# The first load of q in two pieces, and blank matmuls of twice the width

## The chip, the core and the metric

The kernel runs on one core of a Trainium2 chip. A core has engines that work side by side, each with its own queue of instructions: TensorE (PE in the profile; its weight loads are PEld), VectorE (DVE), ScalarE (ACT), GpSimd (POOL) and SyncE (SP), which issues most of the transfers between the chip's main memory and the on-chip memory. Engines wait for each other, and for transfers, by semaphores. The metric is the device time of one execution in microseconds.

## The reference

The program is a linear attention ("cosformer") and then a two-layer network with a leaky ReLU. Batch is 8, heads 8, sequence 576, head size 64, so 4608 tokens of 512 values enter the network; its inner width is 2048.

```python
def phi(x, c, s):                       # c, s: cosine and sine of the position
    r = np.maximum(x, 0.0)
    return np.concatenate([r * c, r * s], axis=-1)
q_p, k_p = phi(q, cos_w, sin_w), phi(k, cos_w, sin_w)
kv  = np.einsum('bhsf,bhsd->bhfd', k_p, v)
z   = np.sum(k_p, axis=2)
num = np.einsum('bhsf,bhfd->bhsd', q_p, kv)
den = np.einsum('bhsf,bhf->bhs', q_p, z)[..., None] + 1e-06
x   = (num / den).transpose(0, 2, 1, 3).reshape(4608, 512)
h   = x @ w_in
out = np.maximum(0.01 * h, h) @ w_out
```

## The kernel before

**Tiles and stages.** For each batch element the first 512 positions lie as 128 partitions by 4 positions (the "main" part); the remaining 64 positions of all elements are gathered into a ninth group of 512 tokens. For each group the kernel builds phi of q and k (DVE and ACT, `phi_half`, L237), turns q round so that its features lie on the partitions (`q_transpose`, L362, in PSUM by TensorE for the first groups), multiplies k with v (`kv_mm`, L285; a column of ones in v gives z), multiplies q with that (`num_half`, L408) and divides (`divide`, L390). The result is turned round again (`x_transpose_half`, L424) and goes through the two layers of the network. The first layer of group 0 is `ffn1` (L451), its second `ffn2` (L470). From group 1 on the network's matmuls are split by a Strassen-like scheme with seven products in place of eight, and the next groups' attention runs between them at positions that tables at the end of the kernel give (L1066 to L1075).

**What sets the order.** The program is written out by hand: each engine carries out its instructions in the order in which the Python code issues them. There is no scheduler that moves them. Before group 1 that order is plain code, L147 to L609.

**The start.** SP issues, in this order, q's first four heads, q's last four, then k's first four, v's first four, k's last, v's last (each 512 KB, `load_main`, L88), and eight loads of the first layer's weights (`load_w1`, L135). The 64 tail positions of k and v go through POOL's queue (L210, L211). The transfers that SP issues use eight semaphores in turn; the ninth waits until the first has landed, and so on.

DVE sets a tile `blank` to zero (L162). `idle(n, ps)` (L166) issues 2n matmuls of that tile, 128 by 128, with itself, 256 columns wide, into a PSUM tile that the next real matmul overwrites or that nobody reads. Their result is zero and is used nowhere: they keep TensorE busy. The kernel calls `idle` in these places:

- L171, 14 (28 matmuls): before anything has landed
- L562, 1 each: behind the eight transposes of q's positions 0 and 1
- L572, 14: inside `kv_half(0, 0)`, before the first matmuls of k and v (tile `ps_kvh`)
- L577, 2: inside the first `num_half` (tile `ps_numh`)
- L586, 2: inside `kv_half(0, 1)`

Between these, DVE and ACT make phi of q from the tile `qst` into `qp` (L239 and L241), four heads at a time: first for the heads of q's first load, then for those of its second. TensorE transposes `qp` (L366), eight heads for each of four positions; DVE and ACT copy that to `qpT` (L247, L249). Then follow phi of k (`kpm`), v (`vmain`) and the matmuls of the two (L290, L299), ACT's copy of them to `kv` (L323), the products with q (L417), the division (L392 to L397) and the transposes of the result (L434).

The line numbers are those of the kernel before; in the changed kernel the lines behind L88 stand two further down and those behind L168 five further down.

Of the kernel before, what the change touches and what calls it, by code (L numbers as in the profile page):

```python
# [13 lines left out]
P = 128  # L14
J = 4
# [3 lines left out]
def kernel(  # L19
# [14 lines left out]
    nc = tc.nc  # L34
# [4 lines left out]
    MAIN = J * P  # L39
# [6 lines left out]
    N2 = MAIN // 2  # L46
# [29 lines left out]
    def psum(where, shape, dtype, name):  # L76
        return ps_of[where].tile(shape, dtype, name=name, tag="ps_" + where)

    st = {}
# [4 lines left out]
    def staged(shape, name, soon=False):  # L84
        p, tag = (early, "early") if soon else (stage, "stage")
        return p.tile(shape, dt.float32, name=name, tag=tag)

    def load_main(nm, src, b, parts=(0, 1), soon=False):  # L88

        if parts[0] == 0:  # L90
            st[nm, b] = staged([P, H, J, D], f"{nm}st", soon)
        lo, hi = 4 * parts[0], 4 * parts[-1] + 4
        nc.sync.dma_start(
            st[nm, b][:, lo:hi],
            src[b, lo:hi, 0:MAIN, :].rearrange("h (p j) d -> p h j d", j=J),
        )

    def load_kvtail(nm, src, b, eng=nc.sync):

# [15 lines left out]
    def load_k(b):  # L115
        load_main("k", k, b)
        load_kvtail("k", k, b)

    def load_v(b):
        load_main("v", v, b)  # L120
        load_kvtail("v", v, b)
# [20 lines left out]
    def load_w2(i):  # L142
        t = staged([P, 4, DM], "w2st", i > 1)
        nc.sync.dma_start(t, w2v[i])
        st["w2", i] = t

    load_main("q", q, 0, (0,))  # L147
    load_main("q", q, 0, (1,))
    load_main("k", k, 0, (0,))
    load_main("v", v, 0, (0,))  # L150
# [10 lines left out]
    blank = const.tile([P, N2], dt.float16, name="blank")  # L161
# [2 lines left out]
    nc.scalar.activation(warm, zero, AF.Sin)  # L164

    def idle(n, ps):  # L166
        for _ in range(2 * n):
            nc.tensor.matmul(ps[:, 0:N2], lhsT=blank[:, 0:P], rhs=blank)  # L168

    ps_idle = psum("s", [P, 2, MAIN], dt.float32, "ps_idle")[:, 0]  # L170
    idle(14, ps_idle)  # L171


# [144 lines left out]
    def kv_half(b, hg, where, blanks=0):  # L318
        ps = psum(where, [P, MAIN], dt.float32, "ps_kvh")
        idle(blanks, ps)  # L320
        ps = ps[:, 0 : 4 * NE]
        kv_mm(b, hg, ps)
        nc.scalar.copy(  # L323
            kv[b][:, 4 * hg : 4 * hg + 4, 0 : NE - 1],
            ps.rearrange("p (h e) -> p h e", h=4)[:, :, 0 : NE - 1],
        )
# [81 lines left out]
    def num_half(g, jp, hg, where, blanks=0):  # L408

        if hg == 0:  # L410
            st["xp", g, jp] = qppool.tile([P, 2, H, D], dt.float16, name="xp", tag="qp")
        ps = psum(where, [P, 2, 512], dt.float32, "ps_numh")
        idle(blanks, ps[:, 0])
        for o in range(2):
            for hh in range(4):
                h = 4 * hg + hh
                nc.tensor.matmul(  # L417
                    ps[:, o, hh * NE : (hh + 1) * NE - 1],
                    lhsT=st["qpT", g, 2 * jp + o][:, h, :],
                    rhs=kv[g][:, h, 0 : NE - 1],  # L420
                )
        divide(ps, st["xp", g, jp][:, :, 4 * hg : 4 * hg + 4, :])
# [243 lines left out]
    ps = psum("n", [P, 2, DM], dt.float32, "ps_o")  # L666
# [22 lines left out]
    ps = psum("h", [P, 2, MAIN], dt.float16, "ps_x")  # L689
# [360 lines left out]
    step = length[2] / 28  # L1050
# [109 lines left out]
```

## Time and profile before

| | |
|---|---|
| median of 3 runs | 271.99 us (271.53 to 272.37) |
| the profiled execution | 271.19 us |
| its span, first to last instruction | 269.4 us |
| PE busy | 263.5 us, 98% of the span |
| DVE busy | 203.8 us, 76% |
| ACT busy | 199.4 us, 74% |
| POOL busy | 13.1 us, 5% |
| first landing of q waited for by DVE until | 4.56 us |

The profile is of one execution. In a row of the timeline the first number is the start in microseconds from the start of the span, the second the time from the first of a group's instructions to the end of its last; then come engine, line, operation, what it writes and reads, its shape, how many there are, and in brackets how long the engine had been idle before and what ended that. SPq is SP's queue: such a row is the issue of a transfer, not the transfer. Matmuls are pipelined: one of 256 columns takes 272 ns from its start to its end, while the next starts 0.11 us after it; so the distance of their starts is what counts. In a row of a tile's transfers, "to landing" is counted from the start of the issue.

### The profile page before, as it was taken

How to read it: one execution, taken by the hardware profiler on the slowest of the kernel's cores; microseconds unless marked ns; L12 is line 12 of the kernel's file. 1: busy time of each engine (PE TensorE's matmuls, PEld its weight loads, DVE VectorE, ACT ScalarE, POOL GpSimd, SP SyncE). 2: the span in 40 equal slices, each digit the busy share in tenths (PEclk: the TensorE clock that was granted, in tenths of full speed). 3: DMA queues.
4: the chain of work that ended last, by engine and by line, in shares of the span. 5: the costliest groups of instructions: out<-in, count | busy, mean ns of one | idle time of the engine just before them, and what ended most of it. 6: DMA issues, size and time to landing. Idle time of an engine off the chain costs nothing.

```text
span 269.4 us, 6623 instructions
## 1 busy us (share of the span) xinstructions
PE 263.5 (98%) x2670; PEld 227.0 (84%) x2670; DVE 203.8 (76%) x452; ACT 199.4 (74%) x329; POOL 13.1 (5%) x25
## 2 busy tenths in 40 slices
PE   8999999999999999999999999999999999999994
PEld 6985455665998989899999999999999899999983
DVE  5875798797967898888879778977687758545652
ACT  8757476696888896978888788878877757666720
POOL 5047001000000000000000000000000000000000
PEclk9999999999999999999999999999999999999999
DMA  6999999979999979958995899669384412200324
GB/s 226 373 392 415 393 386 373 357 170 296 274 252 313 191 195 249 354 116 285 259 254 122 271 239 247 156 202 154 62 142 155 61 41 97 80 0 2 156 41 117
DMA packets 86190, 57.05 MB, mean 212 GB/s; under 512 B 55632, under 2 KB 81232, under 8 KB 85648
## 3 DMA queue, kind: packets, MB, share of 16 engines
q1 hardware_dynamic: 85584, 55.98, 77.0%
q8 instruction: 21, 0.34, 0.6%
q10 hardware_dynamic: 448, 0.39, 0.4%
q0 software_dynamic: 128, 0.26, 0.3%
q14 instruction: 9, 0.07, 0.1%
HBM read 36.70 MB, written 9.44 MB: 171 GB/s over the span
## 4 chain that ended last, share of the span: by engine, by line
PE 76%; DVE 2%; issue 0%
PE ps_o L883 33%; PE ps_h L782 30%; PE ps_h L496 4%; PE ps_num L381 3%; PE ps_h L883 3%; PE ps_kv L290 2%; DVE gs L255 0%; PE ps_kv L299 0%; PE ps_xt L446 0%; DVE xs L397 0%; DVE w L255 0%; DVE wb L255 0%; DVE ob L252 0%; DVE qp L241 0%; DVE kpt L241 0%
## 5 line engine op out<-in xcount | busy, mean ns | idle before, releaser
L883 PEld LDWEIGHTS <-g 128*128 128x128 f16 x648 | 62.7, 98 | 7.2 <-DVE g L252 0.3
L252 DVE TENSOR_TENSOR u<-ps_h,u 128x512 f32<-128x512 f32 x52 | 35.8, 688 | 21.0 <-PE ps_h L782 19.3
L883 PE MATMUL ps_o<-w,g 128*128 128x256 f16 x352 | 51.2, 273 | 0.0
L782 PEld LDWEIGHTS <-w 128*128 128x128 f16 x416 | 44.7, 113 | 1.2
L782 PE MATMUL ps_h<-xT,w 128*128 128x256 f16 x288 | 43.3, 273 | 0.0
L809 ACT ACTIVATE g<-u 128x1024 f16<-128x1024 f32 x26 | 27.5, 1058 | 11.2 <-DVE u L252 10.9
L802 ACT COPY u<-ps_h 128x512 f32<-128x512 f32 x52 | 30.5, 586 | 7.1 <-PE ps_h L782 7.0
L795 ACT ACTIVATE g<-ps_h 128x512 f16<-128x512 f32 x52 | 31.2, 602 | 5.6 <-PE ps_h L782 5.6
L782 PEld LDWEIGHTS <-wa 128*128 128x128 f16 x312 | 33.7, 113 | 1.2
L883 PE MATMUL ps_o<-wb,g 128*128 128x256 f16 x232 | 33.5, 273 | 0.0
L782 PE MATMUL ps_h<-xw,wa 128*128 128x256 f16 x208 | 31.3, 273 | 0.0
L883 PEld LDWEIGHTS <-gs 128*128 128x128 f16 x256 | 24.9, 98 | 2.9
L901 ACT COPY ob<-ps_o 128x512 f32<-128x512 f32 (+1 forms) x32 | 18.1, 565 | 11.9 <-PE ps_o L883 10.6
L496 PE MATMUL ps_h<-xT,w 128*128 128x512 f16 (+1 forms) x104 | 24.7, 363 | 0.0
L397 DVE TENSOR_TENSOR xs<-ps_num,rden 128x512 f16<-128x512 f32 x28 | 19.4, 691 | 1.0
L883 PE MATMUL ps_o<-w,gs 128*128 128x256 f16 x120 | 17.8, 273 | 0.0
L252 DVE TENSOR_TENSOR ob<-ps_o,ob 128x512 f32<-128x512 f32 (+1 forms) x22 | 14.9, 675 | 3.8 <-ACT ob L901 1.9
L883 PE MATMUL ps_o<-wb,gs 128*128 128x256 f16 x120 | 17.5, 273 | 0.0
L792 ACT COPY ps_h<-ps_h 128x512 f32<-128x512 f32 x26 | 14.9, 572 | 2.4 <-PE ps_h L782 1.5
L255 DVE TENSOR_TENSOR gs<-g 128x1024 f16<-128x1024 f16 x16 | 11.0, 688 | 7.3 <-ACT g L809 7.2
L782 PE MATMUL ps_h<-xw,w 128*128 128x256 f16 x104 | 15.6, 273 | 0.0
L782 PE MATMUL ps_h<-xT,wa 128*128 128x256 f16 x104 | 15.6, 273 | 0.0
(116 smaller groups left out, 411.8 us busy)
## 6 DMA issues: line engine op xcount, KB each, us to landing
qst<-in_q_dram SPq DMA_DIRECT2D x7, 1024.0 KB, 6.4
out_dram<-ob SPq DMA_DIRECT2D x14, 512.0 KB, 2.8
kst<-in_k_dram SPq DMA_DIRECT2D x6, 1024.0 KB, 7.1
vst<-in_v_dram SPq DMA_DIRECT2D x6, 1024.0 KB, 7.2
w1st<-in_moe_w_in_dram SPq DMA_DIRECT2D x8, 512.0 KB, 10.5
w2st<-in_moe_w_out_dram SPq DMA_DIRECT2D x4, 1024.0 KB, 12.3
kst<-in_k_dram SPq DMA_DIRECT2D x4, 512.0 KB, 8.1
vst<-in_v_dram SPq DMA_DIRECT2D x4, 512.0 KB, 8.3
```

The lines of the kernel that those rows point to most:

```text
L252: nc.vector.tensor_tensor(out=o, in0=a, in1=b, op=ALU.add)
L255: nc.vector.tensor_tensor(out=o, in0=a, in1=b, op=ALU.subtract)
L381: nc.tensor.matmul(ps[lo:hi, h // 4, (h % 4) * NE : (h % 4 + 1) * NE - 1], lhsT=qpT[:, h, lo:hi], rhs=kv[b][:, h, 0 : NE - 1],)
L397: nc.vector.tensor_tensor(out=xs, in0=ps[:, :, 0 : 4 * NE].rearrange("p a (b e) -> p a b e", e=NE)[:, :, :, 0:D], in1=rden.rearrange("p (a ...
L496: nc.tensor.matmul(ps[:, lo:hi], lhsT=w1[m // 4][c // 2][:, c % 2, m % 4 : 512 : 4], rhs=st["xT", g][:, c, lo:hi], start=(c == 0 and lo == 0),
L782: nc.tensor.matmul(bank[:, p], lhsT=w(c), rhs=st["xb", g][n][:, c], start=(fresh and p == 0 and c == 0), stop=(c == 1), skip_group_check=True,
L792: nc.scalar.copy(bank1[bj], bank1[bi])
L795: nc.scalar.activation(st["g" + nm, g][:, 2 * t : 2 * t + 2], bank1[bi], AF.Lrelu)
L802: nc.scalar.copy(st["u", g, t][:, n], bank1[bi])
L809: nc.scalar.activation(st["gt", g][:, :, 1, 2 * t : 2 * t + 2], st["u", g, t], AF.Lrelu)
L883: nc.tensor.matmul(bank[..., lo:hi], lhsT=st[G2[n], g][:, m, pair * P : (pair + 1) * P], rhs=W2[n](m)[:, lo:hi], start=(fresh and m == 0), ...
L901: nc.scalar.copy(o_at(g, half_, col, pair), bank_of(bi, pair, pair is None))
```

## The change

The first load of q, four heads in one transfer, is issued as two transfers of two heads each; the tile that they fill and the operations that read it are the same. `idle` issues n blank matmuls of 512 columns in place of 2n of 256: the zero tile is read twice over, by a view of it that repeats its 256 columns, and the whole PSUM bank of 512 columns is written.

```diff
-    def load_main(nm, src, b, parts=(0, 1), soon=False):
+    def load_main(nm, src, b, parts=(0, 1), soon=False, cut=1):
 
         if parts[0] == 0:
             st[nm, b] = staged([P, H, J, D], f"{nm}st", soon)
         lo, hi = 4 * parts[0], 4 * parts[-1] + 4
-        nc.sync.dma_start(
-            st[nm, b][:, lo:hi],
-            src[b, lo:hi, 0:MAIN, :].rearrange("h (p j) d -> p h j d", j=J),
-        )
+        step = (hi - lo) // cut
+        for h in range(lo, hi, step):
+            nc.sync.dma_start(
+                st[nm, b][:, h : h + step],
+                src[b, h : h + step, 0:MAIN, :].rearrange("h (p j) d -> p h j d", j=J),
+            )
...
-    load_main("q", q, 0, (0,))
+    load_main("q", q, 0, (0,), cut=2)
...
     def idle(n, ps):
-        for _ in range(2 * n):
-            nc.tensor.matmul(ps[:, 0:N2], lhsT=blank[:, 0:P], rhs=blank)
+        twice = blank[:, None, :].broadcast_to([P, 2, N2])
+        for _ in range(n):
+            nc.tensor.matmul(
+                ps.rearrange("p (a n) -> p a n", a=2), lhsT=blank[:, 0:P], rhs=twice
+            )
```

On SP, at the very start of the program, before (`DMAHW0_49` is the first of the eight semaphores of SP's transfers, `DMAHW1_49` the second, and so on):

```order
L93 DMA qst<-in_q_dram 128x4x256 x2
L93 DMA kst<-in_k_dram 128x4x256
L93 DMA vst<-in_v_dram 128x4x256
L93 DMA kst<-in_k_dram 128x4x256
L93 DMA vst<-in_v_dram 128x4x256
L140 DMA w1st<-in_moe_w_in_dram 128x2x512 x2
L140 DMA w1st<-in_moe_w_in_dram 128x2x512 [waits DMAHW0_49]
L140 DMA w1st<-in_moe_w_in_dram 128x2x512 [waits DMAHW1_49]
```

And the same place on SP after the change:

```order
L95 DMA qst<-in_q_dram 128x2x256 x2
L95 DMA qst<-in_q_dram 128x4x256
L95 DMA kst<-in_k_dram 128x4x256
L95 DMA vst<-in_v_dram 128x4x256
L95 DMA kst<-in_k_dram 128x4x256
L95 DMA vst<-in_v_dram 128x4x256
L142 DMA w1st<-in_moe_w_in_dram 128x2x512
L142 DMA w1st<-in_moe_w_in_dram 128x2x512 [waits DMAHW0_49]
L142 DMA w1st<-in_moe_w_in_dram 128x2x512 [waits DMAHW1_49]
L142 DMA w1st<-in_moe_w_in_dram 128x2x512 [waits DMAHW2_49]
```

One transfer more stands ahead of all others, so the second of the weight loads is now the ninth transfer and the first that waits for a landing, that of q's first piece.

On PE, behind the eight transposes of q's position 0, before:

```order
L366 LDWEIGHTS qp
L366 MATMUL ps_qt<-ident,qp 128x128
L168 LDWEIGHTS blank
L168 MATMUL ps_idle<-blank 128x256
L168 LDWEIGHTS blank
L168 MATMUL ps_idle<-blank 128x256
L366 LDWEIGHTS qp
```

On PE after the change, in the same place:

```order
L371 LDWEIGHTS qp
L371 MATMUL ps_qt<-ident,qp 128x128
L171 LDWEIGHTS blank
L171 MATMUL ps_idle<-blank 128x512
L371 LDWEIGHTS qp
```

Two blank matmuls with a weight load each became one; the 28 of the start and the 28 before the first matmuls of k and v became 14 in the same way.

On DVE, the first operations that read q, before (`Activation_49` is ACT's semaphore):

```order
L229 CAST vmain<-ones 128x32x2 [waits DVE_49]
L224 TENSOR_SCALAR vtail<-ones,odd 128x4x2 x2
L241 TENSOR_SCALAR qp<-qst,cos_t 128x4x64 [waits DMAHW0_49,Activation_49]
L241 TENSOR_SCALAR qp<-qst,sin_t 128x4x64 [waits Activation_49]
L241 TENSOR_SCALAR qp<-qst,cos_t 128x4x64
```

And on DVE after the change:

```order
L234 CAST vmain<-ones 128x32x2 [waits DVE_49]
L229 TENSOR_SCALAR vtail<-ones,odd 128x4x2 x2
L246 TENSOR_SCALAR qp<-qst,cos_t 128x4x64 [waits DMAHW1_49,DMAHW0_49,Activation_49]
L246 TENSOR_SCALAR qp<-qst,sin_t 128x4x64 [waits Activation_49]
L246 TENSOR_SCALAR qp<-qst,cos_t 128x4x64
```

The first operation on q waits for both pieces; the order of the operations is as it was.

## The prediction

> **What bounds the kernel now.** I read the span and the engines' shares first, then four stretches of the span with each engine's busy time, then what PE and its weight loads waited for after the first 5 us, and then the first 17 us in order of time, because everything that the change touches lies there.
>
> ```profile
> span 269.4 us, 6623 instructions
> PE 263.5 (98%) x2670; PEld 227.0 (84%) x2670; DVE 203.8 (76%) x452; ACT 199.4 (74%) x329; POOL 13.1 (5%) x25
> ...
> 0.00:5.40 5.40, 4.31 (x21) 3.07 (x22) 2.35 (x15) 4.32 (x9) 3.68 (x14) 1.00 0.63 206
> 5.40:17.00 11.60, 11.29 (x164) 10.00 (x163) 10.33 (x34) 8.77 (x19) 2.72 (x5) 1.00 1.04 373
> 17.00:265.00 248.00, 247.44 (x2481) 213.57 (x2479) 190.49 (x403) 186.34 (x303) 6.67 (x7) 1.00 0.78 206
> ...
> PE ps_num L381 <- DVE xs L397: 0.5, 1, 0.5
> ```
>
> The columns of a stretch are its length, busy PE, PEld, DVE, ACT and POOL, the clock, the DMA share and GB/s. From 17 us to 265 us PE is busy for 247.44 of 248.00 us: no other engine can be the bound there, and work that PE starts earlier or later at 17 us ends earlier or later by as much. PE's longest wait behind that point, 0.5 us on a DVE result, hangs itself on matmuls that PE did before. So the change is worth what it moves PE's work at 17 us, and nothing else. The start goes like this:
>
> ```profile
> 0.73 1.02 SPq L93 DMA_DIRECT2D qst<-in_q_dram  x2
> 1.09 5.33 PE L168 MATMUL ps_idle<-blank 128*128 128x256 f16 x28 [1.09 <-DVE blank L162]
> 4.56 0.35 DVE L241 TENSOR_SCALAR qp<-qst,cos_t 128x256 f16<-128x256 f32 x1 [1.73 <-DMA qst<-in_q_dram]
> 4.71 9.46 SPq L140 DMA_DIRECT2D w1st<-in_moe_w_in_dram  x8
> 6.14 0.35 DVE L241 TENSOR_SCALAR qp<-qst,sin_t 128x256 f16<-128x256 f32 x1
> 6.26 0.69 PE L366 MATMUL ps_qt<-ident,qp 128*128 128x128 f16 x8
> 6.55 0.11 PEld L366 LDWEIGHTS <-qp 128*128 128x128 f16 x2
> 7.00 0.61 PE L366 MATMUL ps_qt<-ident,qp 128*128 128x128 f16 x8
> 7.45 0.38 PE L168 MATMUL ps_idle<-blank 128*128 128x256 f16 x2
> 8.56 3.22 PE L168 MATMUL ps_kvh<-blank 128*128 128x256 f16 x28
> 8.76 1.01 ACT L247 COPY qpT<-ps_qt 128x1024 f16<-128x1024 f16 x1 [0.75 <-PE ps_qt L366]
> 11.28 0.61 ACT L247 CAST vmain<-vst 128x512 f16<-128x512 f32 x1
> 11.62 0.73 PE L290 MATMUL ps_kvh<-vmain,kpm 128*128 128x65 f16 x16
> 13.06 1.17 POOL L249 CAST vmain<-vst 128x512 f16<-128x512 f32 x2 [8.64 <-DMA vst<-in_v_dram]
> 17.18 0.39 PE L434 MATMUL ps_xth<-ident,xp 128*128 128x128 f16 x4
> ```
>
> While q's first half is fetched, PE runs 28 blank matmuls. DVE and ACT start on q when the load has landed (DVE waited 1.73 us for it); the DVE operation at 6.14 ends at 6.49 and lets PE begin the fifth transpose (its weights load at 6.55). Then PE runs without a break into the 28 blanks at 8.56, which fill the wait for k and v. ACT's copy at 8.76 comes straight from the last transposes, and from it ACT works through to the cast that ends at 11.89, for which the ninth of the matmuls at 11.62 waits. From there k, v and the divisions lead to 17.18.
>
> So the first 17 us have two reins: PE's own columns (blanks, then transposes), and the landing of q. They lie very close together.
>
> **The first load in two.** Its rows and those of the loads behind it:
>
> ```profile
> L93 SPq DMA_DIRECT2D qst<-in_q_dram x2: 471/482/492, 0.7 to 1.3; - x2
> DMA to landing us min/median/max: 3.7/4.1/4.5
> ...
> L93 SPq DMA_DIRECT2D kst<-in_k_dram x2: 507/543/579, 1.8 to 2.9; - x2
> DMA to landing us min/median/max: 6.8/7.8/8.8
> ...
> L93 SPq DMA_DIRECT2D vst<-in_v_dram x2: 508/830/1151, 2.3 to 3.5; - x2
> DMA to landing us min/median/max: 8.0/8.7/9.5
> ```
>
> Issue plus landing time gives 4.4 us for q's first half (0.73 + 3.7), 5.8 for its second (1.26 + 4.5), 11.7 for the second half of k (2.90 + 8.8) and 13.0 for that of v (3.52 + 9.5). Issues follow each other by about 0.54 us, but the last two loads land 1.3 us apart: the transfers are the slow part and the issues run ahead of them. SP gets one more issue. It moves the five loads behind it by some 0.54 us, and the eight w1 loads, but none of these is waited for at the issue: the first w1 issue stands from 4.71 and the eight take 9.46 us, because the queue is full or an earlier load has to land. After the change the second and third w1 load wait for the landing of q's two pieces (by 4.5 us), which are there before those issues' turn. So the issue itself is hidden, by the backlog of transfers; without that backlog it would cost up to 0.54 us.
>
> What the second piece costs in transfer has no row; the nearest is one load of 1 MB that lands 2.6 us after the load before it, as much as two of 512 KB at 1.3 us each, so that a piece more costs under 0.1 us, the rounding of these rows; I take 0.07:
>
> ```profile
> L144 SPq DMA_DIRECT2D w2st<-in_moe_w_out_dram x1: 341/341/341, 16.7 to 16.7; - x1
> DMA to landing us min/median/max: 12.8/12.8/12.8
> ...
> L93 SPq DMA_DIRECT2D qst<-in_q_dram x1: 379/379/379, 18.0 to 18.0; - x1
> DMA to landing us min/median/max: 14.1/14.1/14.1
> ```
>
> (16.66 + 12.8 is 29.5, 17.99 + 14.1 is 32.1.) A gain is possible too, since the transfers start slowly:
>
> ```profile
> 1.80:2.20 0.40, 0.40 (x4) 0.28 (x3) 0.26 (x2) 0.39 (x2) 0.40 (x2) 1.00 0.57 100
> 2.20:2.60 0.40, 0.40 (x4) 0.28 (x3) 0.37 (x4) 0.28 (x3) 0.40 (x2) 1.00 0.72 195
> 2.60:3.00 0.40, 0.40 (x4) 0.28 (x3) 0.23 (x2) 0.38 (x3) 0.40 (x1) 1.00 0.97 310
> 3.00:3.40 0.40, 0.40 (x3) 0.28 (x2) 0.00 (x0) 0.40 (x1) 0.40 (x2) 1.00 1.07 381
> ```
>
> Against 381 GB/s the first three stretches lose 0.4 × (281 + 186 + 71) / 381 = 0.56 us, with engines idle (share 0.57 and 0.72). If that is the time in which the load's descriptors are handed out engine by engine, half a load halves it: −0.28 us. So q lands between −0.28 + 0.07 = −0.21 and +0.07 us; the far end, if the piece came as late as its issue, is +0.61.
>
> On the path: DVE's operation at 6.14 moves with q, and so does PE's fifth transpose, but only down to where the fourth ends. The first begins at 6.26 and they follow each other by (7.45 − 7.00) / 8 = 0.056 us, so the fifth can't begin before 6.48, while it now begins at 6.55. An earlier q is therefore worth at most 0.07 us, whatever it gains beyond; a later one costs its full delay. I take the earlier landing, since the slow start is a row of this very load: −0.07 us; the other end is +0.07.
>
> The Trainium skill speaks against the cut: DMA: Bandwidth & Descriptors, in its anatomy of one DMA, fits a fixed cost of about 2.0 us to each DMA (for those that GpSimd issues) and asks for large ones; paid in series it would make 274.0 us of this. The landings 1.3 us apart don't bear that out for loads in a queue, where such a cost overlaps.
>
> The first operations on q, one on DVE and one on ACT, get a third semaphore to wait for. Behind them stand all the others on q. The first piece signals earlier than the second, so the extra wait is over when the second comes: 0.
>
> **Blanks of 512 columns.** Their rows:
>
> ```profile
> L168 PE MATMUL ps_idle<-blank x32: 272/421/421, 1.1 to 7.6; 128*128 128x256 f16 x32
> L168 PE MATMUL ps_kvh<-blank x32: 270/272/273, 8.6 to 13.8; 128*128 128x256 f16 x32
> ...
> 1.30:5.30 4.00, 4.00 (x20) 2.85 (x19) 0.00 (x0) 1.00 0.83 270
> ...
> 30.61 3.62 PE L476 MATMUL ps_o<-w,g 128*128 128x512 f16 x16
> 34.06 0.61 PE L366 MATMUL ps_qt<-ident,qp 128*128 128x128 f16 x8
> ```
>
> Until about 5.4 us a blank takes 421 ns and they follow by some 0.21 us; then 272 ns and 0.11: the array starts at half speed (the clock column reads 1.00 there all the same; its record begins only later). At full speed the 28 blanks of the second wait take (11.62 − 8.56) / 28 = 0.1093 us each, 3.06 us; 512 columns take (34.06 − 30.61) / 16 = 0.2156 us, and 14 of them 3.02 us. That is −0.04 us, but the ninth matmul of k and v still waits for ACT at 11.89, so it is worth 0. In the slow part the columns alone count: 14 × 0.427 is 28 × 0.213, so the first block ends where it did, less 0.01 us for its fast part. Lone pairs between the transposes become one each: −0.005 us twice, on the path. The pairs and fours behind 12 us lie ahead of waits for ACT and DVE: 0. The weight loads that fall away lie beside the matmuls: 0. Sum of this half: −0.02 us.
>
> **The sum.** −0.07 − 0.02 is −0.09 us, with ends of −0.1 and +0.6. The profiled execution took 271.19 us for its span of 269.4, with 1.8 outside; it would take 271.1. The median of the runs is 0.8 us above that execution and even the fastest run (271.53) 0.34 above, so executions differ by more than the change is worth. Against the median: 271.9 us, no change. About 0.3% (0.8 us) is what a measurement of this kernel can tell from none.
>
> **The rivals.**
>
> *The second piece lands late (slower).* If its descriptors aren't ready when the first piece has been moved, q lands later by an issue, 0.54 us, and 0.07: 272.6. If the pieces went one after the other, the second would repeat what the first spends beside its transfer, 3.7 − 1.3 = 2.4 us: 274.4. It decides from +0.8 us on. The transfers that land 1.3 us apart speak against it. Chance 0.12, more than half of it slower.
>
> *The clock counts matmuls, not time (slower).* The speed rose at about 5.4 us, when 20 blanks had gone. If it needs that many, the 14 wide ones all run slowly, to 1.09 + 14 × 0.427 = 7.06 us instead of 6.26, and seven transposes too, at 0.056 more each: +1.2 us less the 0.07 of slack, 273.1 us. It decides if the rise comes 1.6 us later than now. The one rise in the trace tells neither way. Chance 0.09. TensorE: Matmul & The Clock Gate of the Trainium skill (Part 1, on the clock gate) says that a window of about 3.4 us of activity decides and not a number of matmuls; by that the time stays.
>
> *The rise comes early in every execution (faster).* The profiled execution beat every run by 0.34 us or more. If it is a lucky one, in which the speed rose before the blanks were out, and others run all 28 slowly, to 7.06, they lose the 0.8 us by which the median lies above it. Should blanks with half as many joints raise the clock early each time, the runs come down to 271.1. For it speaks only the size of the gap; against it, that the slow blanks follow each other without idle time already. Chance 0.19, nearly all faster.
>
> **How the numbers follow.** The forecast has 0.60, of which the scatter of executions puts 0.03 beyond the bound on each side. The late piece gives 0.05 to no change and 0.07 to slower, the counted matmuls 0.02 and 0.07, the early rise 0.17 to faster and 0.02 to no change. So faster 0.20, same 0.63, slower 0.17. The range takes in the early rise with 0.1 us (271.0) and goes most of the way to the counted matmuls (272.9); outside lie the serial pieces, most of the counted case and the tail of the early rise.
>
> **What the profile after would show.** Two issues at the start where there was one, and all loads landing within 0.2 us of before; DVE's first operation on q at 4.4 to 4.6 us; the first transpose at 6.25 and the fifth at 6.48; 14 blanks 0.216 us apart at 8.5; k and v's first matmul near 11.5, the ninth still behind ACT; the transposes of 17.18 at 17.1. The forecast is wrong if blanks are still slow behind 6 us in one kernel only, or if q lands after 4.6 us.

## The result and the profile after

The changed kernel takes 273.81 us (median of 15 executions, 272.81 to 278.41) where the kernel before takes 271.70 us (15 executions beside them, 271.14 to 272.39). The ratio is 1.0089, with a 95% interval of 1.0067 to 1.0111: slower by 2.1 us. A ratio in this document leaves out executions more than 1.5% above the fastest of their kernel: here the one at 278.41, below three of the cut alone (276.56 to 277.20) and one of three heads and one (278.49). The prediction was no change, 271.9 us, with a range of 271.0 to 272.9.

The executions fall into two groups. Ten lie at 272.81 to 274.66 us, with a granted clock of 0.997 to 1.0 over the span; of the other five, four lie at 275.92 to 276.80 with a clock of 0.992 to 0.994. The profile is of one of those four, 276.27 us:

```profile
span 274.5 us, 6557 instructions
PE 265.7 (97%) x2636; PEld 224.6 (82%) x2636; DVE 205.4 (75%) x452; ACT 199.6 (73%) x329; POOL 13.6 (5%) x25
```

The start of the changed kernel in order of time, in the columns of the prediction's second fence:

```profile
0.73 1.49 SPq L95 DMA_DIRECT2D qst<-in_q_dram  x3
1.09 5.74 PE L171 MATMUL ps_idle<-blank 128*128 128x512 f16 x14 [1.09 <-DVE blank L164]
4.41 0.35 DVE L246 TENSOR_SCALAR qp<-qst,cos_t 128x256 f16<-128x256 f32 x1 [1.58 <-ACT warm L223]
6.66 0.39 PE L371 MATMUL ps_qt<-ident,qp 128*128 128x128 f16 x4
8.49 0.35 DVE L246 TENSOR_SCALAR qp<-qst,cos_t 128x256 f16<-128x256 f32 x1 [2.68 <-DMA qst<-in_q_dram]
9.16 0.40 PE L371 MATMUL ps_qt<-ident,qp 128*128 128x128 f16 x4 [2.12 <-DVE qp L246]
15.86 0.67 PE L295 MATMUL ps_kvh<-vmain,kpm 128*128 128x65 f16 x16
21.22 1.18 PE L465 MATMUL ps_h<-xT,w 128*128 128x256 f16 x8
```

The first operation on q starts at 4.41 us, 0.15 earlier than before. But DVE then waits 2.68 us, until 8.49, for the next load, q's second half, and PE's fifth transpose comes at 9.16 instead of 6.55, after 2.12 us without work. The landings of q's three loads, from the rows of their tile:

```profile
L95 SPq DMA_DIRECT2D qst<-in_q_dram x3: 455/463/469, 0.7 to 1.8; - x3
...
DMA to landing us min/median/max: 2.8/3.0/6.7
```

With the issues at 0.73, 1.26 and 1.75 the two pieces landed at 3.6 and 4.3 us, and the second half at 8.5; before, it landed at 5.8. The last column of the stretches, GB/s, shows what the transfer engines did in between. The columns ahead of it are the length, busy PE, PEld, DVE, ACT and POOL, the clock and the DMA share. Before:

```profile
4.00:4.50 0.50, 0.50 (x5) 0.33 (x3) 0.00 (x0) 0.35 (x2) 0.42 (x1) 1.00 1.04 363
4.50:5.00 0.50, 0.50 (x4) 0.38 (x3) 0.44 (x2) 0.45 (x2) 0.00 (x0) 1.00 1.10 389
```

And after:

```profile
4.00:4.50 0.50, 0.50 (x3) 0.17 (x2) 0.09 (x1) 0.46 (x3) 0.42 (x1) 1.00 0.87 248
4.50:5.00 0.50, 0.50 (x3) 0.23 (x2) 0.50 (x3) 0.50 (x2) 0.00 (x0) 1.00 0.81 233
```

The first matmul of the network, which has a row of its own in both kernels, tells how much of the loss lies ahead of it. Before:

```profile
16.17 1.07 PE L460 MATMUL ps_h<-xT,w 128*128 128x256 f16 x7
```

From 16.17 to 21.22 is 5.05 us; the spans, 269.4 and 274.5, differ by 5.1. So all of it is lost in the start. It falls into three parts: 2.61 us up to the fifth transpose (6.55 to 9.16); another 1.63 up to the first matmul of k and v (11.62 to 15.86, less 2.61); and 0.81 from there. The second part fits the clock, in two stretches of the changed kernel:

```profile
6.27:9.68 3.41, 1.29 (x14) 0.77 (x13) 1.19 (x5) 1.19 (x3) 0.00 (x0) 1.00 0.98 305
9.68:13.10 3.42, 3.42 (x28) 2.87 (x27) 2.09 (x6) 1.34 (x3) 0.00 (x0) 0.50 1.08 384
```

From 9.68 to 13.10 us the granted clock is 0.50, and half of 3.42 us is 1.71 us; the cut alone, profiled below without that fall, lost nothing there. In the third part DVE's operations on k run at twice their duration (0.69 us for 0.35) from 15.73 us on, while POOL casts weights beside them; the rows show the two together, and no run tried to separate them.

By this an execution without the lower clock should have the first part alone. The ten of the first group have a median of 273.4 us, 1.7 above the kernel before, which is less than the 2.61 of this profile. The four of the second lie around 276.1, another 2.7 us up, about what the second and third part make together (2.4). Only one execution was profiled, so what the others lost, and where, is inferred from their times and clocks.

### The profile page after: what moved, and what is told of

Its sections match the earlier page's. It is cut to its first block, busy times and chain, and to the rows that moved or that the text cites. A ratio compares the mean times of both kernels' runs of the same rounds, so it can differ in the third digit from the quotient of the medians.

```text
span 274.5 us, 6557 instructions
## 1 busy us (share of the span) xinstructions
PE 265.7 (97%) x2636; PEld 224.6 (82%) x2636; DVE 205.4 (75%) x452; ACT 199.6 (73%) x329; POOL 13.6 (5%) x25
## 4 chain that ended last, share of the span: by engine, by line
PE 74%; DVE 2%; issue 0%
PE ps_o L888 33%; PE ps_h L787 29%; PE ps_h L501 4%; PE ps_num L386 3%; PE ps_h L888 3%; PE ps_kv L295 2%; DVE gs L260 0%; PE ps_kv L304 0%; PE ps_xt L451 0%; DVE xs L402 0%; DVE w L260 0%; DVE wb L260 0%; DVE ob L257 0%; DVE qp L246 0%; DVE kpt L246 0%
```

## The experiments

**Each half of the change alone.** The changed kernel with the narrow blanks of before:

```diff
-        twice = blank[:, None, :].broadcast_to([P, 2, N2])
-        for _ in range(n):
-            nc.tensor.matmul(ps.rearrange("p (a n) -> p a n", a=2), lhsT=blank[:, 0:P], rhs=twice)
+        for _ in range(2 * n):
+            nc.tensor.matmul(ps[:, 0:N2], lhsT=blank[:, 0:P], rhs=blank)
```

> Only the cut of q's first load; blanks as before (28 of 256 columns). Theory 1 (the issue that the cut adds moves q's second half back to POOL's tail loads, and it lands some 2.7 us late): the second half of q lands at about 8.4 us as in the changed kernel, first operation on it at about 8.5 us, time 272.8 to 276.5 with the same spread as the change. Theory 2 (the wide blanks cost the time): as before, 271.7 within 0.5, second half of q at 5.8 us.

The median of 10 is 273.26 us (272.24 to 277.20). The ratio, 1.0036 (1.0011 to 1.0060), is that of the seven up to 273.86. The start of the profiled execution (273.37 us) in order of time:

```profile
8.72 0.40 PE L368 MATMUL ps_qt<-ident,qp 128*128 128x128 f16 x4 [2.45 <-DVE qp L243]
...
13.79 0.73 PE L292 MATMUL ps_kvh<-vmain,kpm 128*128 128x65 f16 x16
...
18.34 1.18 PE L462 MATMUL ps_h<-xT,w 128*128 128x256 f16 x8
```

Without the clock's loss the delay is passed on unchanged: the fifth transpose is 2.17 us late, the matmuls of k and v 2.17 (13.79 for 11.62), the network 2.17 (18.34 for 16.17), and the span (271.6) 2.2. The cut alone makes the late load. The seven have a median of 272.55 us, though, only 0.7 above the kernel before beside them (271.81): how late the load came in the others isn't on record.

The changed kernel with q's first load whole:

```diff
-    load_main("q", q, 0, (0,), cut=2)
+    load_main("q", q, 0, (0,))
```

> Only the blanks of 512 columns, half as many; q's first load whole as before. Theory 1: q's second half at 5.8 us, the speed of the array as before, time 271.7 within 0.4. Theory 2 (wide blanks raise the clock later, or lose it): 273 or more, and the array slow at some stretch behind 6.5 us.

272.45 us (271.24 to 274.02, 10 executions), ratio 1.0027 (1.0001 to 1.0052). q landed as before, but in the profiled execution v came later, and PE waited for it, as the order of time shows:

```profile
12.42 0.67 PE L295 MATMUL ps_kvh<-vmain,kpm 128*128 128x65 f16 x16 [0.46 <-DVE vmain L254]
```

Is that the wide blanks, or the scatter of loads? The kernel before with only the 28 blanks of the first wait made into 14 wide ones:

```diff
-    idle(14, ps_idle)
+    twice = blank[:, None, :].broadcast_to([P, 2, N2])
+    for _ in range(14):
+        nc.tensor.matmul(ps_idle.rearrange("p (a n) -> p a n", a=2), lhsT=blank[:, 0:P], rhs=twice)
```

> The kernel before, with only its first 28 blanks as 14 wide ones; q's first load whole, all other blanks narrow. If the wide blanks cost something by the way in which the array's speed rises, it is seen here: 272.2 to 272.6. If not: 271.5 to 272.0.

272.27 us (271.88 to 272.59, 12 executions), ratio 1.0003 (0.9982 to 1.0025). The ratio shows no difference, but the median lies 0.5 us above that of the kernel before (271.80), within what was expected of a cost; in the profile the first matmul of the network comes at 16.22 us, for 16.17 before. Over all executions the medians of the cut alone and of the wide blanks alone lie 1.45 and 0.64 us above their kernel before, that of the change 2.1. So the cut is the larger part; what the wide blanks cost, and by which of them, stays open.

**Is it GpSimd's tail loads?** The first reason that I formed was that the four tail loads of POOL's queue come between SP's second and third load. The changed kernel with five more fills of a scratch tile on POOL ahead of them, which moves the issue of the first from 1.81 to 3.05 us:

```diff
+    scratch = begin.tile([P, P], dt.float32, name="scratch")
+    for _ in range(5):
+        nc.gpsimd.memset(scratch, 0.0)
     load_kvtail("k", k, 0, nc.gpsimd)
```

> The change, with POOL's loads of the tails of k and v put off by about 1 us (five small memsets of an unused tile ahead of them); nothing else. Theory 1: q's second half is ahead of the tail loads again and lands at 5.5 to 5.9 us; k's first half then takes the collision; time 271.3 to 272.2. Rival (the cut as such, one more transfer in SP's queue, makes q's second half late, POOL has no part): it still lands behind 8 us and the time stays at 272.8 or more.

273.16 us (272.50 to 274.31, 10 executions), ratio 1.0041 (1.0009 to 1.0072). q's second half still came 5.4 us after its issue, at 7.2 us, which is neither the 5.5 to 5.9 of the theory nor the 8 of the rival, and the second piece of its first half came later than before, at 1.26 + 3.9 = 5.2. The row of the tile:

```profile
DMA to landing us min/median/max: 2.8/3.9/5.4
```

The next run takes POOL's queue out altogether; its tails go through SP's, behind the first load of k and that of v:

```diff
     load_main("k", k, 0, (0,))
+    load_kvtail("k", k, 0)
     load_main("v", v, 0, (0,))
+    load_kvtail("v", v, 0)
...
-    load_kvtail("k", k, 0, nc.gpsimd)
-    load_kvtail("v", v, 0, nc.gpsimd)
```

> The change, with the tails of k and v loaded through SP's queue (k's behind k's first half, v's behind v's first half) and not through POOL's. Theory 1 (what is loaded through POOL's queue beside SP's third load makes that one late): with one queue only, q's second half lands at 5.3 to 5.9 us, PE has no wait of 2 us between its transposes, time 271.2 to 272.4. Rival (the third load of SP's queue is late whatever POOL does): it lands behind 7 us, time 272.5 or more.

273.16 us (272.50 to 274.68, 10 executions), ratio 1.0051 (1.0021 to 1.0081). The second half of q landed 6.1 us after its issue, at 7.9 us, with nothing in POOL's queue. The landings from the tile's rows, and the GB/s in the last column of the stretches between 3.5 and 5.5 us:

```profile
DMA to landing us min/median/max: 2.7/2.9/6.1
...
3.50:4.00 0.50, 0.50 (x2) 0.15 (x1) 0.00 (x0) 0.50 (x1) 0.00 (x0) 1.00 1.03 205
4.00:4.50 0.50, 0.50 (x3) 0.18 (x2) 0.23 (x1) 0.49 (x3) 0.00 (x0) 1.00 0.49 121
4.50:5.00 0.50, 0.50 (x3) 0.23 (x2) 0.50 (x3) 0.50 (x2) 0.00 (x0) 1.00 0.81 264
5.00:5.50 0.50, 0.50 (x3) 0.20 (x2) 0.50 (x3) 0.50 (x2) 0.00 (x0) 1.00 1.07 352
```

While q's second piece ends (it landed at 1.26 + 2.9 = 4.2), and with further loads issued long ago, the transfer engines fall to 121 GB/s and a share of 0.49: about half of the time they move nothing. So the first reason falls: POOL's loads aren't needed for the delay. They do lengthen the thin stretch: in the changed kernel the rate stays under 280 GB/s until 6.5 us, here it is back at 352 from 5.0 on. The same four lines in the kernel before, that is with q's first load whole:

> The kernel before with the tails of k and v through SP's queue. Theory 1: k's first half, which is the third load here and takes the collision in the kernel before (landing at 8.6 us), lands at 7.0 to 7.4 us, and the loads behind it follow in the order of the queue; those are not waited for until 9 us, so the time is 271.3 to 272.0. If POOL's queue has no part, k's first half stays behind 8 us.

271.48 us (270.95 to 272.39, 10 executions), ratio 0.9981 (0.9957 to 1.0006), the best median of all, though the interval takes in no change. k's first half, the third load there, landed 6.5 us after its issue at 1.79, at 8.3 us; had POOL's loads held it up, 7.0 to 7.4 was expected.

**Is it the cut, or any load ahead?** The kernel before, uncut, with a load of 32 KB that nobody reads between q's two halves:

```diff
     load_main("q", q, 0, (0,))
+    tiny = const.tile([P, D], dt.float32, name="tiny")
+    nc.sync.dma_start(tiny, q[0, 0, 0:P, :])
     load_main("q", q, 0, (1,))
```

> The kernel before, q uncut, blanks of 256 columns, with one small unused load (128 rows of 256 bytes) issued between q's two halves: it moves the second half's issue from 1.26 to about 1.8 us, as the cut does. Theory 1: q's second half lands at about 8.4 us, time 272.8 to 276.5. Rival (the cut itself): about 5.9 us and 271.7 to 272.1.

273.19 us (272.58 to 276.22, 10 executions), ratio 1.0062 (1.0029 to 1.0094). The second half, third in the queue again, landed at 1.80 + 5.9 = 7.7 us. So a load of 32 KB in second place does what the cut does, and the bytes aren't the cause. Two reasons were left. By place: the third load is slow, whatever stands ahead of it. By landings: a load's transfers begin only about 1 us after the load two places ahead of it has landed, so that two loads of which the second is short leave the engines idle until the third may begin. They part when the small load comes first:

```diff
+    tiny = const.tile([P, D], dt.float32, name="tiny")
+    nc.sync.dma_start(tiny, q[0, 0, 0:P, :])
     load_main("q", q, 0, (0,))
     load_main("q", q, 0, (1,))
```

> The kernel before with a load of 32 KB that nobody reads issued ahead of q's first half, so that q's halves are second and third in SP's queue. Theory by place (the third load comes slowly, whatever stands ahead of it): q's second half lands at 7.2 to 8.5 us, PE has a gap of 1.5 to 2.5 us before the fifth transpose, 272.8 to 273.5 us. Rival by landings (only two loads of a queue are served at a time, so that the third begins about 1 us after the first has landed): the small load lands before 3.2 us, so q's second half finds its turn while the first half is still coming, and lands at 5.8 to 6.4 us; q's first half lands 0.1 to 0.5 later than before; 271.8 to 272.4 us.

271.88 us (271.67 to 272.87, 10 executions), ratio 0.9988 (0.9963 to 1.0013). The rows of the small load's tile and of q's:

```profile
L148 SPq DMA_DIRECT2D tiny<-in_q_dram x1: 407/407/407, 0.7 to 0.7; - x1
...
DMA to landing us min/median/max: 1.8/1.8/1.8
...
L93 SPq DMA_DIRECT2D qst<-in_q_dram x2: 418/462/507, 1.2 to 1.7; - x2
...
DMA to landing us min/median/max: 3.7/4.1/4.6
```

The first landed at 0.73 + 1.8 = 2.5 us, and the third at 1.66 + 4.6 = 6.3, 1.4 us behind the second (1.20 + 3.7 = 4.9), with no thin stretch (309 GB/s or more between 3.0 and 6.5 us). The third place as such isn't slow; the reason by place falls.

q's first half in four loads:

```diff
-    load_main("q", q, 0, (0,), cut=2)
+    load_main("q", q, 0, (0,), cut=4)
```

> The changed kernel with q's first half in four loads of one head each instead of two; q's second half is the fifth load. Theory by place: the third piece is slow and lands at 6 to 8 us, and since DVE's first operation on q waits for all four, it starts then instead of at 4.4; q's second half comes 1 to 1.5 us behind it; 274 to 276 us. Rival by landings (two at a time): the third piece begins about 1 us after the first has landed (at 2.9), so the four pieces land by 4.8 to 5.5, q's second half by 7 to 8; 273 to 274 us.

273.26 us (272.74 to 274.11, 10 executions), ratio 1.0034 (1.0004 to 1.0065). The rows of q's tile, and the thinnest stretch with GB/s in the last column:

```profile
L95 SPq DMA_DIRECT2D qst<-in_q_dram x5: 403/432/434, 0.7 to 2.6; - x5
...
DMA to landing us min/median/max: 2.1/2.4/4.6
...
4.50:5.00 0.50, 0.50 (x3) 0.22 (x2) 0.39 (x2) 0.41 (x1) 0.00 (x0) 1.00 0.59 119
```

The first of the four landed at 0.74 + 2.1 = 2.8 us, the last at 2.13 + 2.4 = 4.5, where the reason by place had the third at 6 to 8. The fifth load, q's second half, came at 2.60 + 4.6 = 7.2, after a thin half microsecond (119 GB/s).

**The same loads and bytes, shared out otherwise.** The last pair leaves the count of loads, their order and their bytes as in the changed kernel, and only puts one head into the first piece and three into the second, or three and one:

```diff
-        step = (hi - lo) // cut
-        for h in range(lo, hi, step):
+        h = lo
+        for step in cut:
             nc.sync.dma_start(
...
+            h += step
...
-    load_main("q", q, 0, (0,), cut=2)
+    load_main("q", q, 0, (0,), cut=(1, 3))
```

> The changed kernel with q's first four heads in a load of one head and a load of three, instead of two and two: as many loads and bytes, in the same order. Theory by landings (two loads at a time: the third begins about 1 us after the first has landed): the first, of 128 KB, lands at about 2.9 us, so the third may begin at about 3.9, while the second still comes until about 4.5: no stretch between 3.0 and 5.5 us falls under 290 GB/s, q's second half lands at 5.7 to 6.3 us, PE's gap before the fifth transpose is under 0.5 us, and the time is 271.5 to 272.4 us. Rival (one more load ahead costs, however the bytes are shared out): q's second half lands after 7 us and the time is 273.0 to 273.8 us.

272.05 us (271.60 to 273.46, 11 executions), ratio 1.0017 (1.0001 to 1.0033). The rows of the same two views, for one head and three:

```profile
L97 SPq DMA_DIRECT2D qst<-in_q_dram x3: 407/418/488, 0.7 to 1.7; - x3
...
DMA to landing us min/median/max: 2.0/3.4/4.3
...
3.50:4.00 0.50, 0.50 (x2) 0.15 (x1) 0.00 (x0) 0.50 (x1) 0.50 (x2) 1.00 1.08 367
4.00:4.50 0.50, 0.50 (x4) 0.24 (x3) 0.00 (x0) 0.35 (x2) 0.42 (x1) 1.00 1.04 334
4.50:5.00 0.50, 0.50 (x4) 0.25 (x3) 0.25 (x1) 0.27 (x1) 0.00 (x0) 1.00 1.05 371
```

> The changed kernel with q's first four heads in a load of three heads and a load of one. Theory by landings: the first lands at about 4.0 us, the second at about 4.4, so the third can't begin before about 5.0: a stretch between 4.0 and 5.5 us falls under 200 GB/s, q's second half lands at 6.8 to 8.5 us, PE's gap before the fifth transpose is 1 to 2.5 us, and the time is 272.9 to 273.8 us. Rival (the cost is that of one more load, however the bytes are shared out): the same time as with one head and three, within 0.3 us.

274.24 us (273.21 to 278.49, 7 executions), ratio 1.0092 (1.0060 to 1.0124). And for three heads and one, from a profile of the slowest execution:

```profile
L97 SPq DMA_DIRECT2D qst<-in_q_dram x3: 433/471/471, 0.7 to 1.8; - x3
...
DMA to landing us min/median/max: 3.0/3.1/6.8
...
3.50:4.00 0.50, 0.50 (x2) 0.15 (x1) 0.00 (x0) 0.50 (x1) 0.50 (x2) 1.00 0.47 146
4.00:4.50 0.50, 0.50 (x3) 0.17 (x2) 0.16 (x1) 0.49 (x3) 0.42 (x1) 1.00 0.57 182
4.50:5.00 0.50, 0.50 (x3) 0.23 (x2) 0.50 (x3) 0.50 (x2) 0.00 (x0) 1.00 0.67 211
```

With the short piece first the rate holds (334 to 371 GB/s), q's second half lands at 6.0 us and most of the loss is gone. With the short piece last the rate falls to 146, the second half lands at 8.6 and the kernel is as slow as the changed one (its profiled execution has the lower clock too, but only from 9.73 us on, behind these rows). There were misses: with three and one the landing came 0.1 us and the median 0.4 us above their ranges, and PE's gap with one and three was 0.8 us where under 0.5 was expected, since there the clock rose at 4.0 us and the blanks were out by 5.9. The landings together:

| kernel | KB of the first two loads | first landed | second landed | third landed |
|---|---|---|---|---|
| short load first | 32, 512 | 2.5 | 4.9 | 6.3 |
| one and three | 128, 384 | 2.8 | 4.6 | 6.0 |
| three and one | 384, 128 | 3.9 | 4.2 | 8.6 |
| the change | 256, 256 | 3.6 | 4.3 | 8.5 |
| short load second | 512, 32 | 4.7 | 4.9 | 7.7 |
| the kernel before | 512, 512 | 4.5 | 5.8 | 8.6 (k's first half) |

The third load is on time, 1.4 us behind the second, where the first landed 1.8 us or more ahead of the second. It is late, 2.8 to 4.4 us behind, where the first landed 0.7 us or less ahead. The kernel before lies between (1.3 us ahead) and is late too (2.8 us), but its third load isn't waited for so early. Apart from that row, the size of the second load sorts the kernels just as well (384 KB and more on time, 256 KB and less late), so the runs don't tell whether the landing of the first load or the length of the second decides. The 1 us of the reason by landings is a fit to these times; the profile doesn't show which load a packet belongs to.

**Two ways round it.** If PE had something to do, would the loss shrink? The changed kernel with 24 wide blanks in the first wait instead of 14:

```diff
-    idle(14, ps_idle)
+    idle(24, ps_idle)
```

> The change, with 24 wide blanks in the first wait instead of 14, so that PE is busy to about 9 us while q's second half is late. The late landing stays; if the runs above 274 us come from a clock that falls back after PE's wait of 2 us, none is above 274 here and the median is 272.5 to 273.4. If they come from the loads themselves, as many runs as before (about one in three) are above 274.

274.83 us (274.16 to 275.24, 9 executions), ratio 1.0099 (1.0070 to 1.0129). That is neither of the two that were expected: all nine lie above 274. No execution shows the lower clock any more (0.996 and more over the span), but the blanks themselves now hold PE up: all the transposes come behind them, the first four too, as the order of time shows:

```profile
8.34 0.63 PE L371 MATMUL ps_qt<-ident,qp 128*128 128x128 f16 x8
...
18.62 1.18 PE L465 MATMUL ps_h<-xT,w 128*128 128x256 f16 x8
```

The first matmul of the network comes 2.45 us later than before (16.17). The span (272.9 us) is longer by 3.5; the other 1.1 us lie behind that matmul and aren't explained.

The other way is to take q's second half out of SP's queue and have ACT issue it:

```diff
-    load_main("q", q, 0, (1,))
+    load_main("q", q, 0, (1,), eng=nc.scalar)
```

> The changed kernel, but q's second half is issued by ACT, as the first instruction of its queue, instead of being third in SP's queue; on SP k's first half is third now. Theory (the third load of a queue comes slowly at the start, whichever it is): q's second half lands at 5.5 to 6.2 us, DVE's operation on it follows within 0.1 us, PE's gap before the fifth transpose shrinks from 2.1 us to under 0.3, k's first half lands at 7 to 8.7, and the time is that of the kernel before or a few tenths above, 271.5 to 272.3 us. Rival (three loads in flight are too many for the transfer engines, from whatever queue): q's second half still lands after 7 us and the time stays near 273.2.

274.58 us (274.20 to 275.69, 10 executions), ratio 1.0096 (1.0069 to 1.0123). The second half landed early, at 0.74 + 4.5 = 5.3 us, as the theory had it, but in between it pushed back the second piece of the first half, to 1.26 + 4.7 = 6.0 us. The rows of q's tile, and the fifth transpose in the order of time:

```profile
L95 SPq DMA_DIRECT2D qst<-in_q_dram x2: 454/462/471, 0.7 to 1.3; - x2
...
L95 ACTq DMA_DIRECT2D qst<-in_q_dram x1: 489/489/489, 0.7 to 0.7; - x1
...
DMA to landing us min/median/max: 3.5/4.5/4.7
...
8.10 0.40 PE L371 MATMUL ps_qt<-ident,qp 128*128 128x128 f16 x4 [0.92 <-DVE qp L246]
```

DVE's first operation waits for both pieces, starts at 6.11 instead of 4.41, and the fifth transpose comes at 8.10, 1.55 us later than before. By the first matmul of the network (19.16 us) the delay is 3.0. So the landing was as expected, the time not.

## Why the prediction was wrong

- **The step that failed** is "So the issue itself is hidden, by the backlog of transfers; without that backlog it would cost up to 0.54 us." There is no backlog that serves the third load in time: it and two more had been issued by 3.4 us, but behind the two short pieces the engines ran down to 248 and 233 GB/s, where before they had 363 and 389. The price was not 0.54 us but 2.7 (8.5 for 5.8). I took the landings 1.3 us apart for a queue without gaps; they come from later loads of 512 KB, which don't show what happens behind short ones. The profile of before held a hint that I passed over: k's first half, its third load, landed 2.8 us behind the second (1.80 + 6.8 = 8.6, against 5.8), not 1.3.
- **The pieces themselves** came when forecast, but not for the reason given. "q lands between −0.28 + 0.07 = −0.21 and +0.07 us": 4.29 for 4.47, −0.18. The slow start wasn't halved, though: the changed kernel's three stretches from 1.8 us on have 51, 179 and 356 GB/s and lose 0.4 × (330 + 202 + 25) / 381 = 0.58 us, for 0.56 before. So the agreement is luck. The gain stayed without effect, as said. What I called the far end, +0.61, was that of the pieces; the load behind them wasn't priced at all. So "DVE's operation at 6.14 moves with q" moved it with the wrong load: it reads q's second half.
- **The rival of the late piece** had a similar size (+0.6 to +2.4) and another mechanism. In the runs with two pieces in SP's queue the second landed at 4.2 to 4.6 us, save in two: 5.2 with POOL's loads put off, and 6.0 beside ACT's load. The page of the Trainium skill that I weighed against it, DMA: Bandwidth & Descriptors (anatomy of one DMA), gives a fixed cost of about 2.0 us to each DMA that GpSimd issues; the measured loss of 2.1 us is near that, but one head and three, with as many transfers, cost 0.3 us, so it isn't a cost that each transfer adds here.
- **The blanks.** Those of the first wait, made wide, cost nothing by the ratio (1.0003, 0.9982 to 1.0025), as worked out; the wide blanks all together may cost some tenths (1.0027, 1.0001 to 1.0052), against the −0.02 us worked out. The first transpose came at 6.66 us in the changed kernel instead of 6.25, as in that execution the clock rose at 6.27 and not at 5.4; with the cut alone it rose at 4.68.
- **The clock.** That matmuls are counted isn't borne out: with 14 wide or 28 narrow blanks alike it rose somewhere between 4.0 and 6.5 us in the profiles. What I hadn't thought of is that it falls again. **The early rise** isn't borne out either: no execution with wide blanks comes under the range of the kernel before.

What stays open: how the lateness comes about inside the chip, and whether the limit is that of a queue or of the core. A late beginning is not all of it. A load's semaphore has sixteen updates, as many as there are transfer engines. For q's second half they come at 5.2 to 5.8 us in the kernel before. In the changed kernel the eighth is there at 5.9, half a microsecond later, but the last at 8.5; with the tails on SP fifteen are there by 6.6 and the last at 7.9. So in these two profiles the larger part of the delay is a spread between the sixteen parts of one load, for which no run shows a reason.

## What to carry to other kernels

Before a load is cut at the start of a kernel, look at the load behind it, not at the pieces: with a short load in second place, the transfer engines here fell to 121 to 248 GB/s although more loads had been issued. Where one must be cut, the short piece belongs first and the long one behind it; here that cost 0.3 us instead of 2.1, and gained nothing over the whole load. And a landing that a queue's later loads repeat every 1.3 us is no price for the first three.

## What the runs showed of the hardware

**The clock falls behind a period in which PE worked little, and a gap's length alone doesn't decide.** In every profile the clock's record changes in steps of 3.41 us from its rise. The two rows on the clock in the section on the result are one such period and the next. The same two stretches of the changed kernel with its tails on SP, where the clock also fell:

```profile
5.42:8.84 3.42, 1.50 (x14) 0.85 (x13) 1.22 (x5) 1.10 (x4) 0.00 (x0) 1.00 1.07 344
8.84:12.25 3.41, 3.41 (x29) 2.87 (x27) 1.85 (x5) 1.24 (x2) 0.00 (x0) 0.50 1.00 310
```

The period of three heads and one ahead of its fall at 9.73:

```profile
6.32:9.73 3.41, 1.19 (x12) 0.66 (x11) 1.11 (x5) 1.11 (x3) 0.00 (x0) 1.00 1.03 359
```

The cut alone, where it didn't fall:

```profile
4.68:8.09 3.41, 1.60 (x17) 1.28 (x14) 1.08 (x5) 0.97 (x4) 0.00 (x0) 1.00 0.98 321
8.09:11.51 3.42, 2.79 (x40) 2.67 (x41) 3.05 (x9) 2.73 (x5) 0.00 (x0) 1.00 1.04 361
```

And the kernel before with the short load second, where it didn't either:

```profile
4.53:7.94 3.41, 1.67 (x17) 1.36 (x15) 1.65 (x6) 1.55 (x4) 0.00 (x0) 1.00 0.95 313
```

PE busy for 1.19, 1.29 and 1.50 us of a period: half speed in the next. Busy for 1.60 and 1.67: full speed. One period at the end of the changed kernel doesn't fit a bound between these, since behind 1.46 us the clock stayed up:

```profile
269.10:272.51 3.41, 1.46 (x22) 1.29 (x19) 0.94 (x3) 0.27 (x1) 0.00 (x0) 1.00 0.80 212
272.51:274.48 1.97, 0.00 (x0) 0.00 (x0) 0.00 (x0) 0.00 (x0) 0.00 (x0) 1.00 0.11 32
```

So near 1.5 us the busy time doesn't settle it. Nor can it be told from the idle time within the period, which in these is one gap. A gap's whole length doesn't decide: 2.45 us in the cut alone left the clock up, and there the gap lay across the end of a period; 2.12 us in the changed kernel, within one, brought it down. So much the same gap costs some 2.5 us or nothing, by where the period happens to stand. That fits the two groups of executions, of which only single ones were profiled. The Trainium skill, TensorE: Matmul & The Clock Gate ("Why this matters for your kernels"), asks for no gaps above about 3 us and names one window of idle time as the condition. The steps of 3.41 us bear out a window; the 3 us are not borne out: here a period with 1.50 us of work and a gap of 1.92 us was enough to fall.

**A short second load makes the third one late.** What the table of landings shows wasn't expected: with the tails on SP, where four loads more had been issued by 4.3 us, the transfer engines were left at a share of 0.49 and 121 GB/s when the first two loads ended close together (3.5 and 4.2 us).
